# An HGRN recurrence with capacity-limited experts behind it: gathers, scatters, zero blocks and copied blocks in another order

## The chip, the core and the metric

The kernel runs on one core of one Trainium2 chip. The metric is the time of one execution on the device in microseconds, the median of several runs; lower is better. TensorE (PE) multiplies matrices, VectorE (DVE), ScalarE (ACT) and GpSimd (POOL) work elementwise, and SyncE (SP) issues most of the transfers. Each engine takes its own instructions in the order of the program and waits at semaphores for the others. Sixteen DMA engines carry every transfer between HBM (DRAM) and SBUF; PSUM is where TensorE writes.

## What is computed

The reference, cut to what matters. B, S, D = 4, 5056, 256, so N = 20224 tokens; E = 8 experts, F = 1024, capacity 80.

```python
sig = 1 / (1 + exp(-f_logit))
f = lower_bound + (1 - lower_bound) * sig
h = 0
for t in range(S):                     # per batch row and channel
    h = f[:, t] * h + (1 - f[:, t]) * x[:, t]
    y[:, t] = h
x = y.reshape(B * S, D)
logits = x @ w_gate
expert_idx = argmax(logits, axis=1)
gate_w = softmax(logits)[expert_idx]   # of each token, its own expert's
out = zeros((N, D))
for e in range(E):
    tok_idx = where(expert_idx == e)
    if len(tok_idx) > capacity:
        tok_idx = the capacity tokens with the largest gate_w
    out[tok_idx] = gate_w[tok_idx] * (relu(x[tok_idx] @ w1[e]) @ w2[e])
```

So at most 640 of the 20224 rows of the output are not zero; the other rows must be written as zeros.

## The kernel before

The first stage goes over 40 units of tokens (10 groups of 512 in each of the 4 batch rows). A unit loads 512 KB of `f_logit` and 512 KB of `x` into two of the eight ring slots (`ring`, 128x1024 f32 each), ScalarE takes the sigmoid, GpSimd multiplies it with `x` (`enter`), TensorE turns both, VectorE scans along time into `h_all`, which stays in SBUF whole, and TensorE makes the logits. In between, `copied` and `clear` write zeros to the output: `clear(source)` sends a tile of zeros from SBUF to the next 512 KB of `out`, `copied()` copies the first 512 KB of `out`, already zero, to the next 512 KB of `out`. One `clear(early)` and eleven `copied()` belong to this stage.

The second stage selects: VectorE and ScalarE rank candidates of each expert, TensorE counts and places them, and `trow` holds the token numbers of 8 x 80 slots. While it runs, SP brings the first seven halves of weights and writes more zeros. A half is 512 KB, half of `w1[e]` or of `w2[e]`, and takes slots 1 to 7 of the ring in turn (`half`); the order of the halves is `halves_of`. A half can be loaded once the half that lies seven before it in the order has been used up by TensorE.

The third stage, `experts`, is an order written out by hand; no planner moves anything. In it:

- `gather(e)` copies the 80 columns of `h_all` of expert e into `X[e]`, 24 on VectorE, 32 on ScalarE, 24 on GpSimd, each after loading the token numbers into the engine's registers; the tile pool `xp` has three buffers. `scaled(e)` multiplies `X[e]` on GpSimd.
- `hidden(e)` is 64 products with the two halves of `w1[e]` into two PSUM tiles; `relu(e, ps)` brings one to SBUF on ScalarE and one on VectorE; `result(e)` is 64 products with the two halves of `w2[e]`, and VectorE copies the result into `turned_y`, a band of 384 columns.
- `more(1)` issues two halves, and before `again` a `copied()` behind each half while blocks are left.
- `read_slots` loads slot numbers and gate values from DRAM, `rows_of` is a chain of 14 small VectorE instructions that makes from them the output rows (`goal`) and the factors (`gates`).
- `finish(t)` turns 128 columns of `turned_y` back (TensorE) and multiplies them by `gates` (VectorE) into `rows[0]`, which lies in ring slot 0; `scatter(t)` is an indirect DMA from GpSimd that writes these 128 rows to `out`. There are five (NT = 5).

The loop in short, with `finish` and `scatter` as soon as their rows are there but not ahead of e = 3 and e = 5:

```python
for e in range(E):
    if e and e + 2 < E: gather(e + 2)
    if e + 1 < E: ps = hidden(e + 1); relu(e + 1, ps); more(1)
    result(e); more(1)
    if e and e + 2 < E: scaled(e + 2)
    # e == 1: read_slots   e == 3: rows_of   then finish(..), scatter(..)
```

The branch `tc.If(unsure > 0)` at the end does the selection again in full and is not entered with these inputs.

Of the kernel before, what the change touches and what calls it, by code (L numbers as in the profile page):

```python
# [26 lines left out]
def kernel(  # L27
# [59 lines left out]
    def slot(i, name):  # L87
        return ring[i].tile([P, R * D], F32, name=name, tag="buf")
# [77 lines left out]
    with tc.tile_pool(name="gsm", bufs=1) as gsm:  # L166
# [228 lines left out]
        with tc.tile_pool(name="plg", bufs=1, space=PSUM) as plg, \  # L395
             tc.tile_pool(name="plt", bufs=1, space=PSUM) as plt:
            with tc.tile_pool(name="pss", bufs=2, space=PSUM) as pss, \
                 tc.tile_pool(name="psu", bufs=3, space=PSUM) as psu:
                for n in range(-AHEAD, n_unit):
                    unit(load, n + AHEAD)  # L400
                    m = n + AHEAD
                    if m == 1:
                        small_loads()
                    if m == 3:
                        clear(early)
                    elif 3 < m < TURN and m % 4 == 3:
                        copied()
                    elif m == n_unit - 1:
                        for _ in range(3):
                            copied()  # L410
                    unit(gate, n + 2)
                    if n == 0:
                        scaled_gate()
                    unit(enter, n + 2)
                    unit(turn_s, n + 1)
                    unit(turn_u, n + 1)
                    if n == n_unit - 2:
                        exponentials(0, LAST - 1)
                    unit(decay, n + 1)
                    unit(scan, n)  # L420
                    if n > 1 and n % B == 1:
                        aside(n // B - 1)
                    if n == n_unit - 3:
                        assert len(jobs) == 4
                    some_of(1 if n < TURN or n >= n_unit - 3 else 2 if n < n_unit - 1 else 0)
                    if n == n_unit - 2:
                        exponentials(LAST - 1, LAST)
                        summed(0, 4)
                        valued(0, 4, nc.gpsimd)
                    unit(logits, n - 1)  # L430
                    if n > 0 and n % B == 0:
                        g = n // B - 1
                        jobs.append(lambda g=g: by_token(g))
                        if g % 2 or g >= LAST - 1:
                            g0 = g - 1 if g < LAST - 1 else g
                            jobs += [lambda g0=g0, g=g: shifted(g0, g + 1),
                                     lambda g0=g0, g=g: equals(g0, g + 1),
                                     lambda g0=g0, g=g: choice(
                                         g0, g + 1, nc.gpsimd if g < LAST - 1 else nc.vector)]
# [48 lines left out]
                nc.vector.match_replace(out=src, in_to_replace=top, in_values=src,  # L488
                                        imm_value=NONE)

    order = [(1, 0), (2, 0), (1, 1)]
    for e in range(1, E):
        order += ([(1, e + 1)] if e + 1 < E else []) + [(2, e)]
    halves_of = [(which, e, i) for which, e in order for i in range(2)]
    used = [0]
# [19 lines left out]
        return t  # L515

    w_sb = {}
    SELECTING = 14
    for k, key in enumerate(halves_of[:NSLOT - 1]):
        if k % 2:  # L520
            copied()
        w_sb[key] = half(*key)
    for _ in range(SELECTING):
        copied()

    def columns_of(pool, at):
        ids = pool.tile([P, at.shape[1]], F32, name="ids")
# [175 lines left out]
    def experts(again):  # L703
        with tc.tile_pool(name="xp", bufs=3) as xp, \
# [7 lines left out]
            late = list(halves_of if again else halves_of[NSLOT - 1:])  # L712
            X, HID = {}, {}
            turned_y = yp.tile([P, DC, YR], F32, name="turned_y")
            rows = []

            def gather(e):
                X[e] = xp.tile([P, DC, K], F32, name="xe", tag="xe")
# [74 lines left out]
                nc.vector.tensor_scalar_mul(rows[0][:, t % R], t_ps, gates[:, ds(t, 1)])  # L793

            def scatter(t):
                nc.gpsimd.indirect_dma_start(  # L796
                    out=out, out_offset=bass.IndirectOffsetOnAxis(ap=goal[:, ds(t, 1)], axis=0),
                    in_=rows[0][:, t % R], in_offset=None, bounds_check=N - 1, oob_is_err=False)

            def more(m):  # L800
                for _ in range(2 * m):
# [13 lines left out]
                busy(psm, 5, "total")  # L815
            gather(1)
            scaled(1)
            ps = hidden(0)
            relu(0, ps)
            more(1)  # L820
            gather(2)
            scaled(2)
            if not again:
                total = psm.tile([1, 4], F32, name="total", tag="total")
                nc.tensor.matmul(total, ones, doubts[:, :4], start=True, stop=True)
            done = put_out = 0
            for e in range(E):
                if e and e + 2 < E:
                    gather(e + 2)
                if e + 1 < E:  # L830
                    ps = hidden(e + 1)
                    relu(e + 1, ps)
                    more(1)
                result(e)
                more(1)
                if e and e + 2 < E:
                    scaled(e + 2)
                if e == 1 and not again:
                    read_slots()
                    found = consts.tile([1, 1], F32, name="found")  # L840
                    nc.vector.tensor_reduce(found, total, AX.X, ALU.add)
                    nc.vector.tensor_copy(doubt, found)
                if e == 3 and not again:
                    rows_of(consts)
                while e >= 3 and (done + 1) * P <= (e + 1) * K:
                    finish(done)
                    done += 1
                while e + 3 >= E and put_out < done:
                    scatter(put_out)
                    put_out += 1  # L850
            assert put_out == NT
# [93 lines left out]
```

## Time and profile before

| what | value |
|---|---|
| median of 3 runs | 230.9 us (229.79 to 231.42) |
| the profiled execution | 230.06 us |
| its span, first to last instruction | 228.3 us |
| granted TensorE clock, mean | 0.947 |
| busy in the span: PE, DVE, ACT, POOL | 179.4, 160.3, 133.5, 140.3 us |
| moved by DMA | 80.66 MB, mean 353 GB/s |

Times in the rows below are microseconds from the start of the span of that one execution. A name such as L747 is a line of the kernel. A busy time of an engine is the union of its instructions; a DMA share is the mean busy share of the 16 DMA engines.

### The profile page before, as it was taken

What the parts mean: (1) busy time and instruction counts of PE and PEld (TensorE: products, weight loads), DVE (VectorE), ACT (ScalarE), POOL (GpSimd) and SP (SyncE); (2) the same over time, 40 slices, a digit from 0 to 9 for tenths busy, and PEclk for the clock granted to TensorE, in tenths of its full rate; (3) what the DMA queues carried; (4) which work ended last, traced back from release to release, by engine and by line L of the source; (5) the groups of instructions that cost most, each with busy time, mean ns of one, the idle gap of its engine ahead of it and who ended that gap; (6) DMA issues with size and microseconds to landing.
All of it is one profiled execution on the core that took longest, in us unless ns stands there. A gap on an engine that the chain in (4) does not pass through costs nothing. (4 is left out here: it accounts for less than half of the span.)

```text
span 228.3 us, 7296 instructions
## 1 busy us (share of the span) xinstructions
PE 179.4 (79%) x2452; PEld 149.5 (66%) x2452; DVE 160.3 (70%) x404; ACT 133.5 (58%) x423; POOL 140.3 (61%) x283
## 2 busy tenths in 40 slices
PE   0699899989998999899989758888957554998500
PEld 0598687867877787678767524578947453987400
DVE  5289878999989998999899999555353414652200
ACT  4288878777977888879788433466653260240000
POOL 4868779788978896889786632566555160052311
PEclk9999999999999999999999988997999987799955
DMA  6999999999999999999999999998999999397110
GB/s 232 335 422 414 414 409 420 408 412 411 392 416 404 411 376 414 417 409 384 411 455 358 425 434 375 353 333 296 332 400 451 401 334 394 127 366 279 41 44 26
DMA packets 20727, 80.66 MB, mean 353 GB/s; under 512 B 4409, under 2 KB 4409, under 8 KB 20057
## 3 DMA queue, kind: packets, MB, share of 16 engines
q1 hardware_dynamic: 20440, 79.46, 89.5%
q0 software_dynamic: 240, 0.66, 0.8%
q8 instruction: 21, 0.34, 0.7%
q14 instruction: 26, 0.20, 0.3%
HBM read 78.92 MB, written 21.37 MB: 439 GB/s over the span
## 5 line engine op out<-in xcount | busy, mean ns | idle before, releaser
L239 POOL TENSOR_TENSOR x_t<-f_t,x_t 128x1024 f32<-128x1024 f32 x40 | 94.9, 2374 | 22.1 <-DMA x_t<-in_x_dram 11.8
L270 DVE TENSOR_TENSOR_SCAN h_all<-h_all,up 128x512 f32<-128x512 f32 (+1 forms) x80 | 96.0, 1244 | 8.8 <-PE up L253 4.2
L262 ACT ACTIVATE h_all<-sp,nomlb 128x512 f32<-128x512 f32 (+1 forms) x80 | 50.1, 677 | 14.8 <-PE sp L245 11.8
L245 PE MATMUL sp<-ident,f_t 128*128 128x128 f32 x320 | 46.0, 289 | 7.0 <-ACT f_t L235 5.6
L235 ACT ACTIVATE f_t<-f_t 128x1024 f32<-128x1024 f32 x40 | 42.4, 1059 | 12.4 <-DMA f_t<-in_f_logit_dram 9.5
L253 PE MATMUL up<-ident,x_t 128*128 128x128 f32 x320 | 45.1, 283 | 4.0 <-DVE h_all L270 2.9
L245 PEld LDWEIGHTS sp<-ident,f_t 128*128 128x128 f32 x320 | 36.4, 147 | 15.1 <-issue 12.7
L253 PEld LDWEIGHTS up<-ident,x_t 128*128 128x128 f32 x320 | 37.2, 145 | 6.9 <-DVE h_all L270 4.4
L725 ACT COPY xe<-h_all 128x2 f32 x256 | 25.4, 190 | 18.5 <-issue 11.5
L747 PE MATMUL h_ps<-xe,w_sb 128*64 128x80 f32 x512 | 28.1, 273 | 7.4 <-DMA w_sb<-in_moe_w_dram 5.4
L725 POOL COPY xe<-h_all 128x2 f32 x192 | 24.5, 189 | 15.1 <-PE kept L679 6.0
L747 PEld LDWEIGHTS h_ps<-xe,w_sb 128*64 128x64 f32 x512 | 26.6, 186 | 9.6 <-DMA w_sb<-in_moe_w_dram 4.3
L725 DVE COPY xe<-h_all 128x2 f32 x192 | 22.6, 173 | 12.9 <-issue 10.7
L283 PE MATMUL lg<-h_all,wg 128*32 128x128 f32 (+1 forms) x640 | 26.5, 282 | 0.6 <-ACT ls L292 0.6
L769 PE MATMUL y_ps<-hid,w_sb 128*64 128x80 f32 x480 | 21.5, 247 | 3.5 <-DMA w_sb<-in_moe_w_dram 3.5
L769 PEld LDWEIGHTS y_ps<-hid,w_sb 128*64 128x64 f32 x480 | 19.9, 149 | 4.2 <-DMA w_sb<-in_moe_w_dram 3.4
L283 PEld LDWEIGHTS lg<-h_all,wg 128*32 128x32 f32 x640 | 15.4, 108 | 7.0 <-issue 4.9
L729 POOL TENSOR_TENSOR xe<-xe,omlb 128x160 f32<-128x160 f32 x8 | 3.6, 454 | 23.6 <-DVE xe L725 17.2
L755 ACT ACTIVATE hid<-h_ps 128x320 f32<-128x320 f32 x8 | 3.5, 434 | 21.7 <-issue 16.5
L796 POOL DMA_INDIRECT out_dram<-y,goal x5 | 5.1, 1023 | 12.7 <-DMA out_dram<-y,goal 11.9
L782 DVE COPY turned_y<-y_ps 128x160 f32<-128x160 f32 (+1 forms) x7 | 2.2, 318 | 14.5 <-PE y_ps L769 14.5
L307 PE MATMUL lt<-ident,ls 128*128 128x128 f32 (+1 forms) x40 | 7.5, 310 | 4.3 <-ACT ls L292 4.3
(132 smaller groups left out, 113.9 us busy)
## 6 DMA issues: line engine op xcount, KB each, us to landing
f_t<-in_f_logit_dram SPq DMA_DIRECT2D x40, 512.0 KB, 6.9
x_t<-in_x_dram SPq DMA_DIRECT2D x40, 512.0 KB, 7.1
out_dram<-out_dram SPq DMA_DIRECT2D x38, 512.0 KB, 10.2
w_sb<-in_moe_w_dram SPq DMA_DIRECT2D x31, 512.0 KB, 7.4
out_dram<-h_all SPq DMA_DIRECT2D x1, 512.0 KB, 8.9
w_sb<-in_moe_w_dram SPq DMA_DIRECT2D x2, 256.0 KB, 5.2
out_dram<-out_dram SPq DMA_DIRECT2D x1, 256.0 KB
out_dram<-y,goal POOLq DMA_INDIRECT x5, 3.5
```

What stands on the lines that cost most here:

```text
L235: nc.scalar.activation(s_t, s_t, ACT.Sigmoid, scale=-1.0)
L239: nc.gpsimd.tensor_tensor(u_t, sts[n], u_t, ALU.mult)
L245: nc.tensor.transpose(ps[:, ds(r * P, P)], sts[n][:, r, ds(o * P, P)], ident)
L253: nc.tensor.transpose(ps[:, r::R], uts[n][:, r, ds(o * P, P)], ident)
L262: nc.scalar.activation(columns(n, o).rearrange("p (k r) -> p k r", r=R), sps.pop((n, o)).rearrange("p (r k) -> p k r", r=R)[:, P - run(n / ...
L270: nc.vector.tensor_tensor_scan(h, h, ups.pop((n, o)), h_all[:, o, ds(spot(n - B) + G - 1, 1)] if n >= B else 0.0, ALU.mult, ALU.add)
L283: nc.tensor.matmul(lgs[g][ds(q * LC, LC), b, :k].rearrange("p (m i) -> p m i", i=2), wg[:, o], pairs[:, :, q], start=o == 0, stop=o == DC ...
L307: nc.tensor.transpose(lts[g0][:k, g - g0, j], ls[:, j::R], ident)
L725: copy(X[e][:, :, ds(k + j, 1)], h_all[:, :, ds(v, 1)])
L747: nc.tensor.matmul(h_ps[ds(s * H, H), c], wo[o][:, at:at + J * (H - 1) + 1:J], xt[:, o], start=o == 0, stop=o == DC - 1, skip_group_check= ...
L769: nc.tensor.matmul(ys[o][ds(s * H, H)], halves[c // CH][:, c % CH, ds(o * P + s * H, H)], hid[:, c], start=c == 0, stop=c == FC - 1, skip_ ...
L796: nc.gpsimd.indirect_dma_start(out=out, out_offset=bass.IndirectOffsetOnAxis(ap=goal[:, ds(t, 1)], axis=0), in_=rows[0][:, t % R], in_offs ...
```

## The change

- `gather` runs one expert further ahead: `gather(2)` and `scaled(2)` stand before `hidden(0)`, and in the loop `gather(e + 3)`, `scaled(e + 3)` stand between `hidden(e + 1)` and `result(e)`. `relu(e)` opens the turn of the loop in place of following `hidden(e)` at once.
- `scatter`: the scatters are told not to depend on each other; the last one depends on all others.
- `read_slots` and the flag for the branch move from e = 1 to e = 0, `rows_of` and the first `finish` from e = 3 to e = 2, the first scatters from e = 5 to e = 4.
- Zeros: GpSimd fills `zbuf` (ring slot 0) with zeros at the end of the first stage. The seven first halves are followed by one `copied()` each, and behind the second of them twelve `clear(zbuf)` are put in. Before, three `copied()` stood between the halves and fourteen behind them.
- The order of the halves: `w1[1]` ahead of `w2[0]`; the rest is as before.

```diff
--- before.py
+++ after.py
@@ -415,6 +415,8 @@
                     unit(turn_s, n + 1)
                     unit(turn_u, n + 1)
                     if n == n_unit - 2:
+                        zbuf = slot(0, "zbuf")
+                        nc.gpsimd.memset(zbuf, 0.0)
                         exponentials(0, LAST - 1)
                     unit(decay, n + 1)
                     unit(scan, n)
@@ -488,8 +490,8 @@
                 nc.vector.match_replace(out=src, in_to_replace=top, in_values=src,
                                         imm_value=NONE)
 
-    order = [(1, 0), (2, 0), (1, 1)]
-    for e in range(1, E):
+    order = [(1, 0)]
+    for e in range(E):
         order += ([(1, e + 1)] if e + 1 < E else []) + [(2, e)]
     halves_of = [(which, e, i) for which, e in order for i in range(2)]
     used = [0]
@@ -515,13 +517,13 @@
         return t
 
     w_sb = {}
-    SELECTING = 14
+    RANKING = 12
     for k, key in enumerate(halves_of[:NSLOT - 1]):
-        if k % 2:
-            copied()
         w_sb[key] = half(*key)
-    for _ in range(SELECTING):
         copied()
+        if k == 1:
+            for _ in range(RANKING):
+                clear(zbuf)
 
     def columns_of(pool, at):
         ids = pool.tile([P, at.shape[1]], F32, name="ids")
@@ -712,7 +714,7 @@
             late = list(halves_of if again else halves_of[NSLOT - 1:])
             X, HID = {}, {}
             turned_y = yp.tile([P, DC, YR], F32, name="turned_y")
-            rows = []
+            rows, sent = [], []
 
             def gather(e):
                 X[e] = xp.tile([P, DC, K], F32, name="xe", tag="xe")
@@ -793,9 +795,17 @@
                 nc.vector.tensor_scalar_mul(rows[0][:, t % R], t_ps, gates[:, ds(t, 1)])
 
             def scatter(t):
-                nc.gpsimd.indirect_dma_start(
+
+                sent.append(nc.gpsimd.indirect_dma_start(
                     out=out, out_offset=bass.IndirectOffsetOnAxis(ap=goal[:, ds(t, 1)], axis=0),
-                    in_=rows[0][:, t % R], in_offset=None, bounds_check=N - 1, oob_is_err=False)
+                    in_=rows[0][:, t % R], in_offset=None, bounds_check=N - 1, oob_is_err=False))
+                for other in sent[:-1]:
+                    if t < NT - 1:
+                        tc.declare_no_dep(sent[-1].ins, other.ins, reason="other rows")
+                    else:
+                        tc.add_manual_dep(sent[-1].ins, other.ins.name, mybir.DependencyInfo(
+                            mybir.DependencyClass.Sync, mybir.DependencyReason.DATA),
+                            reason="all rows")
 
             def more(m):
                 for _ in range(2 * m):
@@ -815,37 +825,36 @@
                 busy(psm, 5, "total")
             gather(1)
             scaled(1)
-            ps = hidden(0)
-            relu(0, ps)
-            more(1)
             gather(2)
             scaled(2)
+            ps = hidden(0)
+            more(1)
             if not again:
                 total = psm.tile([1, 4], F32, name="total", tag="total")
                 nc.tensor.matmul(total, ones, doubts[:, :4], start=True, stop=True)
             done = put_out = 0
             for e in range(E):
-                if e and e + 2 < E:
-                    gather(e + 2)
+                relu(e, ps)
                 if e + 1 < E:
                     ps = hidden(e + 1)
-                    relu(e + 1, ps)
                     more(1)
+                if e + 3 < E:
+                    gather(e + 3)
+                    scaled(e + 3)
                 result(e)
                 more(1)
-                if e and e + 2 < E:
-                    scaled(e + 2)
-                if e == 1 and not again:
+                if e == 0 and not again:
                     read_slots()
                     found = consts.tile([1, 1], F32, name="found")
                     nc.vector.tensor_reduce(found, total, AX.X, ALU.add)
                     nc.vector.tensor_copy(doubt, found)
-                if e == 3 and not again:
-                    rows_of(consts)
-                while e >= 3 and (done + 1) * P <= (e + 1) * K:
+                if e == 2:
+                    if not again:
+                        rows_of(consts)
+                while e >= 2 and (done + 1) * P <= (e + 1) * K:
                     finish(done)
                     done += 1
-                while e + 3 >= E and put_out < done:
+                while e + 4 >= E and put_out < done:
                     scatter(put_out)
                     put_out += 1
             assert put_out == NT
```

## Rows read from the trace of the kernel before

**Rows 1.** Stretches: busy us (count) of PE, PEld, DVE, ACT, POOL; clock, DMA share, GB/s.
```profile
100.00:116.00 16.00, 15.48 (x196) 13.19 (x196) 14.84 (x15) 12.94 (x19) 12.51 (x7) 1.00 1.02 402
138.00:154.00 16.00, 13.99 (x144) 9.32 (x142) 10.76 (x76) 7.69 (x72) 7.96 (x54) 0.96 1.01 346
154.00:168.00 14.00, 13.09 (x256) 12.86 (x256) 7.23 (x53) 9.11 (x86) 7.49 (x51) 0.88 0.91 331
175.00:182.00 7.00, 3.16 (x78) 2.70 (x76) 2.51 (x18) 3.22 (x32) 2.77 (x23) 1.00 1.04 428
195.00:200.00 5.00, 5.00 (x119) 5.00 (x116) 3.23 (x25) 1.65 (x14) 0.45 (x1) 0.78 0.28 95
```

**Rows 2.** Waits of SP's queue: who waited for whom, us, times, longest.
```profile
SPq L513 <- PE h_ps L747: 10.0, 2, 7.2
```

**Rows 3.** Timeline of SP's issues: start, us, engine, line, operation, names, count.
```profile
114.22 1.78 SPq L141 DMA_DIRECT2D out_dram<-out_dram  x3
...
190.36 7.94 SPq L513 DMA_DIRECT2D w_sb<-in_moe_w_dram  x2
...
200.28 5.67 SPq L513 DMA_DIRECT2D w_sb<-in_moe_w_dram  x5
```

**Rows 4.** Timeline of TensorE and ScalarE around expert 5; idle before in brackets.
```profile
186.87 3.46 PE L769 MATMUL y_ps<-hid,w_sb 128*64 128x80 f32 x48 [1.96 <-DMA w_sb<-in_moe_w_dram]
...
193.62 0.62 PE L791 MATMUL t_ps<-ident,turned_y 128*128 128x128 f32 x2 [2.91 <-DVE y L793]
...
194.17 3.85 PE L747 MATMUL h_ps<-xe,w_sb 128*64 128x80 f32 x64
...
198.79 3.36 ACT L725 COPY xe<-h_all 128x2 f32 x32 [1.69 <-issue]
...
201.00 2.44 PE L747 MATMUL h_ps<-xe,w_sb 128*64 128x80 f32 x64
```

**Rows 5.** Timeline of the last experts and the scatters.
```profile
208.64 2.38 PE L769 MATMUL y_ps<-hid,w_sb 128*64 128x80 f32 x64
...
211.92 0.48 DVE L793 TENSOR_SCALAR y<-t_ps,gates 128x256 f32<-128x256 f32 x1 [0.53 <-PE t_ps L791]
...
213.94 0.31 PE L769 MATMUL h_ps<-hid,w_sb 128*64 128x80 f32 x4
...
214.94 0.48 DVE L793 TENSOR_SCALAR y<-t_ps,gates 128x256 f32<-128x256 f32 x1 [0.54 <-PE t_ps L791]
...
219.59 0.97 POOL L796 DMA_INDIRECT out_dram<-y,goal  x1 [3.42 <-DMA out_dram<-y,goal]
223.17 0.97 POOL L796 DMA_INDIRECT out_dram<-y,goal  x1 [2.60 <-DMA out_dram<-y,goal]
```

**Rows 6.** The chain that ended last: start, us, what.
```profile
215.20 3.62 DMA out_dram<-y,goal
```

**Rows 7.** The page's DMA issues: engine, operation, count, KB each, median us to landing.
```profile
out_dram<-out_dram SPq DMA_DIRECT2D x38, 512.0 KB, 10.2
...
w_sb<-in_moe_w_dram SPq DMA_DIRECT2D x2, 256.0 KB, 5.2
...
out_dram<-y,goal POOLq DMA_INDIRECT x5, 3.5
```

**Rows 8.** Timeline of GpSimd: a memset at the start, and the end of stage one.
```profile
1.65 1.02 POOL L203 MEMSET h_all<- 128x1024 f32 x1
...
125.21 1.21 POOL L355 TENSOR_TENSOR cand<-cand 128x256 f32<-128x256 f32 x2 [1.63 <-ACT cand L343]
```

**Rows 9.** Timeline of the first experts.
```profile
154.71 4.38 PE L747 MATMUL h_ps<-xe,w_sb 128*64 128x80 f32 x64 [1.02 <-POOL xe L729]
...
155.99 3.13 ACT L725 COPY xe<-h_all 128x2 f32 x32 [1.59 <-issue]
...
158.88 2.74 PE L769 MATMUL y_ps<-hid,w_sb 128*64 128x80 f32 x64
```

**Rows 10.** The tile of the weights: landings of its loads.
```profile
DMA to landing us min/median/max: 4.5/7.1/10.7
```

## The prediction

> **What bounds the kernel now.** I read the table by stretches first. In 100 to 116, as in 138 to 154 and 175 to 182, the sixteen DMA engines are the limit, with a busy share of 1.0; behind 138 no compute engine but TensorE comes near it [rows 1]. Three things there matter. Where only copies of `out` into `out` run (138 to 154) the queue is as busy but moves 346 GB/s, against 402 for loads and 428 for weights and copies mixed. From 154 to 168 the share falls to 0.91. From 195 to 200 it is 0.28. The waits of SP's queue say why the last happens: a half of `w2` waited 7.2 us for `hidden` to give its ring slot back [rows 2]; it stands in the timeline as the pair of issues that took from 190.36 to 198.30 [rows 3]. The engines' timeline shows what held that `hidden`: TensorE stands in order, `result(3)` ended at 190.33, the transposes of `finish(1)` came at 193.62 after a wait of 2.91 for VectorE's first product, which in the code stands behind the chain of `rows_of`, and `hidden(5)` came at 194.17 [rows 4]. Last, the end: the last product of the experts ends at 214.25, and the five scatters go one after the other to 224.14 [rows 5]; a step of the chain of waits is the landing of the one before, 215.20 to 218.82 [rows 6]. So there are three limits in order of time: DMA bandwidth, then the ring of slots with the order on TensorE, then a serial chain of scatters up to 228.3.
>
> **The change part by part.** *The scatters.* Before, each waits for the landing of the one ahead, 3.58 to 4.39 us from start to start [rows 5, 6]. After, t = 0 to 3 wait for no scatter, t = 0 to 2 are issued an expert earlier, and the last waits for all. Held against the old times of the products: the rows of t = 3 are multiplied by 212.40, so with 0.2 us allowed for the hand-over its scatter starts at 212.6; 3.5 us to landing [rows 7] make 216.1; 0.77 from a landing to the next start (218.82 to 219.59) and the last starts at 216.9 in place of 223.17. Its own rows are there at 215.42, so the added wait costs some 1.3 us beside a scatter without one; nothing is queued behind it on GpSimd but the end. Gain 6.3; 5.8 with a landing as long as 4.1 us, 7.5 if the wait cost nothing. What follows the start of the last scatter, 223.17 to 228.3, stays. Were the scatters still serial, the earlier place alone would let three of them end before t = 3 is due, so this term stands on two legs.
>
> *The zeros.* In both kernels 39.5 blocks of 524,288 B are written, 12 of them ahead of the first weights. The other 27.5 are 3 + 14 + 10.5 copies before; after, 7 copies (one behind each of the first seven halves), 12 clears from `zbuf` and 8.5 copies. A block costs 524,288 B over the rate [rows 1]: 1.52 us for copies alone, 1.30 for loads, 1.22 mixed. No row shows clears in a row. Lower bound 1.22, since nothing went through the queue faster over a stretch; upper bound 1.52, a copy, which writes the same bytes and reads them too. I take 1.30, as a clear crosses between SBUF and HBM once, as a load does; the ends move the sum by -1.0 and +2.6. What 138 to 154 moved, 16 x 346 = 5.5 MB, would take 13.8 us at 402: gain 2.2. And as two more blocks go out before the experts start, two copies fewer stand between their weights.
>
> The Trainium skill ("DMA: Bandwidth & Descriptors", Where 436 GB/s comes from) speaks against this gain: it says that between HBM and SBUF a core's share of the HBM, some 358 GB/s, binds. By that a clear would cost 1.46 us (an estimate from the page) and the sum would come out 1.9 us later. The trace does not agree for loads, at 402 GB/s on this one core [rows 1].
>
> *The fill of `zbuf`.* One memset of 128x1024 on GpSimd, behind the last product into `x_t`. The same shape took 1.02 us, and GpSimd stands idle for 1.63 us just there, until ScalarE's exponentials let it go on at 125.21 [rows 8]: nothing on the path; without that cover, 1.0 us on the selection. SP waits for it with the clears and the next five halves behind: it would reach the first clear at about 120 and stands until some 124.6. A copy takes 10.2 us from issue to landing [rows 7], so what was issued by 119 keeps the DMA engines busy to about 129, and they do not run dry. Of those halves the first wanted are `w1[1]`: 129, 12 clears (15.6) and three blocks (3.9) make 148.5, six ahead of `hidden(1)` at 154.71 [rows 9]. So the swap of `w2[0]` and `w1[1]` costs nothing.
>
> *Gathers one expert ahead.* `gather(e+3)` waits for the buffer of `X[e]`, free once `hidden(e)` ends. An expert costs ScalarE 1.69 for registers, 3.36 for 32 columns [rows 4] and one `relu` of under half a microsecond: 5.5 us, eight times from about 146, so to 190, and `hidden(7)` is not wanted before some 196. Behind each gather stand `relu(e+1)` on ScalarE and VectorE, and on VectorE the copy of `y`, for which TensorE's next `result` waits. `relu(0)` moves behind `gather(2)`, which ended at 159.12; without a `relu` ahead it ends some 0.4 sooner, so `relu(0)` is done at 159.2, where `result(0)` started at 158.88 [rows 9]: +0.3, in a stretch where DMA has slack. If cover is gone, the price is one gather, 5.5.
>
> *The order of the rest.* `read_slots` moves from e = 1 to e = 0, `rows_of` and `finish(0)` from e = 3 to e = 2. VectorE's chain then runs behind `result(2)`, where TensorE waits for weights anyway, and one set of transposes, not two, stands ahead of a `hidden`, so none waits for VectorE's product. Of the 3.84 us between `result(3)` and `hidden(5)` [rows 4] that removes some 2.8. It is not added by itself: it shows as the queue's idle time at 195.
>
> *The queue's sum.* The idle time of 154 to 168 is 0.09 x 14 = 1.3 us, that of 195 to 200 is 0.72 x 5 = 3.6 [rows 1]. With the 2.2 above, 7.1. A count from the other side: the last three copies of the first stage were issued by 116.0 [rows 3], the middle one at about 115.4 landing (10.2) at 125.6; behind it come 32 halves and 27.5 blocks, at 1.30 together 77.4 us, so the last weights land at 203.0 in place of some 210.8 (issued near 205.6 [rows 3], 5.2 to landing [rows 7]): 7.8. I take 8, near the count, since the table's stretches leave out 182 to 195. TensorE stood 3.4 us behind the last landing, because `result(6)` ended only at 211.02 [rows 5]; with products in time it should stand a `result` behind, 2.4: 1 more. Together 9.
> What is late next: `hidden(e)` frees a slot, and a half needs at least 4.5 us from issue to landing [rows 10], with three halves (3.9 us) queued meanwhile. So a gap of some 0.6 us in a round, and one fall of the clock: +1.
>
> *Sum.* -6.3 - 9 + 1 = -14.3 on the profiled execution's own 230.06 (its span is 228.3, 1.8 lie around it), so 215.8. The median of the runs is 0.8 above that execution: I say 216.5, with a span of about 214.
>
> **The rivals.** *Only the tail is won.* The queue's gain is lost: clears cost what copies cost, and the ring, not bandwidth, paces the experts, TensorE freeing slots too late as at 195. For it: seven slots hold less than two experts, and SP waited for `h_ps` while DMA stood idle [rows 1, 2]. Against: that wait has a cause which the change takes out. It gives 230.06 - 6.3 + 0.8 = 224.6.
>
> *The clock stays down (the slower case).* The granted clock was 0.88 in 154 to 168 and 0.78 in 195 to 200 [rows 1], a mean of full clock and of its lower level, behind waits of TensorE. Were experts 4 to 7 to run wholly at 1.2 GHz, each `hidden` (2.44 [rows 4]) and `result` (2.38 [rows 5]) would take twice as long: 9.6 us a round in place of the 5.2 that four halves take on the queue, so 4.4 x 4 = 17.6 more, and the time 234. It decides once a round outlasts the queue by 3.6. Against: `hidden(6)`, just behind a wait, took 2.44, and the waits left in a round are some 0.5 us, with one of 3 ahead of `hidden(4)`.
> The Trainium skill ("TensorE: Matmul & The Clock Gate", HAM oscillation) describes just this, a wait for DMA in each tile that puts the clock down every time. The trace agrees in part: the clock fell twice among the experts, but never stayed down for a whole one.
>
> *It does nothing.* The scatters are held by the zeros and not by each other, and as many bytes go through the queue: 231. Against: the start at 219.59 follows the landing of the one ahead, at 218.82, and no zeros are under way by then [rows 5, 6].
>
> **How the numbers follow.** The forecast, 212 to 220: 0.68 (the bounds of a clear, of a landing and of the hidden gathers). Only the tail, 220 to 227: 0.22. Clock down, over 232: 0.05. Nothing: 0.05. To leave out no more than 2 in 10 the range goes on to 225. The three runs lie 0.7% apart, so under 1% cannot be told from no change. Faster 0.90, same 0.05, slower 0.05.
>
> **What will show it.** Right: three scatters started by about 195, the last some 2 to 3 us behind the last product; in 138 to 154 over 390 GB/s; no stretch of share 0.28; the last weights landed by 204. Wrong: under 370 GB/s while clears run, SP waiting over 3 us for `h_ps`, a granted clock under 0.8 through the last four experts, or the copy of `y` late behind VectorE's last gather.

## The result and the profile after

The changed kernel takes 219.05 us (median of four runs, 217.37 to 220.39) against 231.16 for the kernel before beside it (229.79 to 231.42): a ratio of 0.9484, interval 0.9396 to 0.9572. Forecast were 216.5 and a range of 212 to 225. Some executions of one and the same kernel take a few per cent longer than its others; medians and ratios here are of the others. The profiled execution took 217.37, with a span of 215.6; against the 230.06 and 228.3 of before that is 12.7 less, where the sum said 14.3.

First the table by stretches of the changed kernel, with the columns of [rows 1]:

```profile
116.00:138.00 22.00, 17.01 (x173) 11.73 (x170) 20.97 (x47) 13.88 (x32) 14.06 (x23) 0.93 1.01 412
138.00:154.00 16.00, 13.33 (x149) 9.26 (x148) 9.79 (x72) 6.83 (x67) 7.61 (x52) 0.99 1.04 426
154.00:168.00 14.00, 13.07 (x260) 12.57 (x256) 10.12 (x77) 9.73 (x95) 9.87 (x73) 0.88 0.98 389
175.00:182.00 7.00, 3.95 (x94) 3.49 (x95) 3.68 (x21) 3.22 (x33) 3.23 (x24) 1.00 0.99 390
195.00:200.00 5.00, 4.03 (x87) 3.51 (x88) 0.46 (x2) 0.44 (x1) 1.44 (x2) 1.00 0.89 318
200.00:206.00 6.00, 4.66 (x116) 4.21 (x112) 0.59 (x2) 0.44 (x1) 0.00 (x0) 1.00 0.57 198
```

In 138 to 154 the queue moves 426 GB/s in place of 346, and the stretch of share 0.28 is gone: 0.89. What is new is the 0.57 behind 200, and that TensorE, at full clock, is busy for only 4.0 of the 5 us of 195 to 200, where before it had no idle time. The timeline of TensorE there (start, us, what ran, idle before in brackets):

```profile
186.48 0.44 PE L793 MATMUL t_ps<-ident,turned_y 128*128 128x128 f32 x2 [0.42 <-DVE turned_y L784]
186.85 2.44 PE L749 MATMUL h_ps<-xe,w_sb 128*64 128x80 f32 x64
...
192.27 2.46 PE L749 MATMUL h_ps<-xe,w_sb 128*64 128x80 f32 x61
195.02 0.37 PE L749 MATMUL h_ps<-xe,w_sb 128*64 128x80 f32 x3 [0.30 <-issue]
195.23 0.32 PE L771 MATMUL y_ps<-hid,w_sb 128*64 128x80 f32 x2
195.81 0.38 PE L771 MATMUL y_ps<-hid,w_sb 128*64 128x80 f32 x4 [0.25 <-issue]
196.55 0.41 PE L771 MATMUL y_ps<-hid,w_sb 128*64 128x80 f32 x5 [0.37 <-issue]
197.29 2.21 PE L771 MATMUL y_ps<-hid,w_sb 128*64 128x80 f32 x53 [0.34 <-issue]
199.33 2.39 PE L749 MATMUL h_ps<-xe,w_sb 128*64 128x80 f32 x64
...
204.46 0.91 PE L771 MATMUL y_ps<-hid,w_sb 128*64 128x80 f32 x18 [0.92 <-issue]
...
208.27 0.31 PE L771 MATMUL h_ps<-hid,w_sb 128*64 128x80 f32 x4
```

The stall of 2.91 ahead of the transposes [rows 4] is gone: they start at 186.48 and `hidden(5)` at 186.85, 7.3 us earlier. But `hidden(6)` and `result(5)` took 7.0 us, 192.27 to 199.3, where two such groups need 4.8 [rows 4, 5]: behind 61 products TensorE gets them by twos to fives, one batch in some 0.73 us, and the word in the brackets is "issue", a wait for nothing that the profile names. A second stall, 0.92, stands in `result(6)`. I had forecast neither.

The timeline of GpSimd's scatters:

```profile
192.96 1.22 POOL L799 DMA_INDIRECT out_dram<-y,goal  x1 [0.77 <-DMA w_sb<-in_moe_w_dram]
194.48 0.98 POOL L799 DMA_INDIRECT out_dram<-y,goal  x1 [0.30 <-issue]
195.76 0.98 POOL L799 DMA_INDIRECT out_dram<-y,goal  x1 [0.30 <-issue]
207.01 0.97 POOL L799 DMA_INDIRECT out_dram<-y,goal  x1 [10.28 <-DVE y L795]
210.22 0.97 POOL L799 DMA_INDIRECT out_dram<-y,goal  x1 [2.24 <-DVE y L795]
```

Three are issued in a row by 196, and the last starts 1.6 us behind the last product (208.58); before it was 8.9 behind (214.25 to 223.17) [rows 5]. So the 12.7 us are 5.7 by which the products end earlier and 7.3 by which the last scatter stands nearer behind them, less 0.3 behind it (5.4 to the end of the span, before 5.1).

### The profile page after: what moved, and what is told of

It reads as the page before. It is cut to its first block, busy times and chain, and to the rows that moved or that the text cites. A ratio compares the mean times of both kernels' runs of the same rounds, so it can differ in the third digit from the quotient of the medians.

```text
span 215.6 us, 7313 instructions
## 1 busy us (share of the span) xinstructions
PE 177.4 (82%) x2452; PEld 146.8 (68%) x2452; DVE 158.4 (73%) x404; ACT 132.6 (62%) x423; POOL 141.5 (66%) x284
## 4 chain that ended last, share of the span: by engine, by line
PE 35%; DMA 22%; ACT 14%; issue 12%; DVE 10%; SPq 2%; POOL 1%; ACTq 1%; POOLq 0%; DVEq 0%
PE sp L245 12%; DMA w_sb<-in_moe_w_dram 11%; PE up L253 9%; PE lg L283 7%; DMA f_t<-in_f_logit_dram 6%; ACT h_all L262 6%; ACT xe L727 4%; DMA lb<-in_lower_bound_dram 3%; DVE h_all L270 3%; PE lt L307 3%; ACT ls L292 2%; PE y_ps L771 2%; PE h_ps L749 2%; POOL out_dram L799 1%; DVE at L632 1%
## 5 line engine op out<-in xcount | busy, mean ns | idle before, releaser
L245 PE MATMUL sp<-ident,f_t 128*128 128x128 f32 x320 | 45.5, 287 | 7.0 <-ACT f_t L235 5.6
L245 PEld LDWEIGHTS sp<-ident,f_t 128*128 128x128 f32 x320 | 36.0, 145 | 15.1 <-issue 12.7
L727 ACT COPY xe<-h_all 128x2 f32 x256 | 25.4, 191 | 18.8 <-issue 10.3
L749 PE MATMUL h_ps<-xe,w_sb 128*64 128x80 f32 x512 | 27.1, 264 | 6.5 <-DMA w_sb<-in_moe_w_dram 5.0
L749 PEld LDWEIGHTS h_ps<-xe,w_sb 128*64 128x64 f32 x512 | 25.5, 178 | 8.5 <-DMA w_sb<-in_moe_w_dram 4.2
L771 PEld LDWEIGHTS y_ps<-hid,w_sb 128*64 128x64 f32 x480 | 18.7, 138 | 5.5 <-issue 4.6
```

The lines of the kernel that those rows point to most:

```text
L245: nc.tensor.transpose(ps[:, ds(r * P, P)], sts[n][:, r, ds(o * P, P)], ident)
L727: copy(X[e][:, :, ds(k + j, 1)], h_all[:, :, ds(v, 1)])
L749: nc.tensor.matmul(h_ps[ds(s * H, H), c], wo[o][:, at:at + J * (H - 1) + 1:J], xt[:, o], start=o == 0, stop=o == DC - 1, skip_group_check= ...
L771: nc.tensor.matmul(ys[o][ds(s * H, H)], halves[c // CH][:, c % CH, ds(o * P + s * H, H)], hid[:, c], start=c == 0, stop=c == FC - 1, skip_ ...
```

## The experiments

Two questions: what is each part worth, and where does TensorE's shortage of instructions come from? For the second there were two theories. **L** (loads): TensorE's instructions are themselves fetched through the DMA engines, and a fetch queued behind weights comes late. **S** (scatters): the scatters issued in a row take something from TensorE. Each ratio is to the kernel before on the same chip; the first four runs shared a chip, as did the four f and the three g.

**The parts one at a time.** The scatters alone:

```diff
-                nc.gpsimd.indirect_dma_start(
+                sent.append(nc.gpsimd.indirect_dma_start(
...
+                for other in sent[:-1]:
+                    if t < NT - 1:
+                        tc.declare_no_dep(sent[-1].ins, other.ins, reason="other rows")
+                    else:
+                        tc.add_manual_dep(...)
```

> The kernel before with only the scatters freed of each other (the last still waits for all), in their old places. Theory 1, the chain of scatters held the end by itself: last scatter starts near 216.9 in place of 223.2, the time falls by 6.3, ratio 0.973. Rival, the scatters are held by the products or by something else on GpSimd: under 2 us, ratio over 0.99.

Measured: 0.9835 (0.9774 to 0.9895), 225.45 against 228.84; expected was 0.973. In its trace the last scatter starts at 216.60, 6.6 earlier than in the trace of before, as the term said. But here the three scatters in a row (205.67, 207.19, 208.47) fall into `hidden(7)` and `result(6)`, and TensorE's timeline shows the same small batches:

```profile
207.22 0.37 PE L769 MATMUL y_ps<-hid,w_sb 128*64 128x80 f32 x5
207.75 0.41 PE L769 MATMUL y_ps<-hid,w_sb 128*64 128x80 f32 x5 [0.16 <-issue]
```

`result(6)` took 4.5 us in place of 2.38 [rows 5]. These 2 us are lost already within the 6.6. The medians differ by 3.4 only; the profiled execution, 223.82, is the fastest of the four, and the rest of the gap stays unexplained.

The zeros alone (the fill of `zbuf`, the 12 clears and the fewer copies):

```diff
+                        zbuf = slot(0, "zbuf")
+                        nc.gpsimd.memset(zbuf, 0.0)
...
-    SELECTING = 14
+    RANKING = 12
...
-        if k % 2:
-            copied()
...
-    for _ in range(SELECTING):
...
+        if k == 1:
+            for _ in range(RANKING):
+                clear(zbuf)
```

> The kernel before with only the zeros changed: zbuf filled, twelve clears, a copy behind each of the first seven halves. Theory 1, clears cost 1.25 us in place of 1.5 and two copies fewer stand among the weights, but TensorE still stalls ahead of hidden(5) and the scatters still go one by one: 2 to 4 us less, ratio 0.983 to 0.991. Rival, the experts are paced by ring slots and TensorE: no change, ratio 0.997 to 1.003, with more idle DMA.

Measured: 0.9927 (0.9887 to 0.9968), a gain of 1.6 us, under the 2 to 4 of theory 1; 138 to 154 moves 419 GB/s. The faster queue is there, but with the old order of the experts not all of it reaches the end: the transposes ahead of `hidden(5)` still wait 3.03 us for VectorE, at 191.04.

The order alone (gathers one expert ahead, order of halves, `read_slots`, `rows_of` and `finish` an expert earlier; scatters issued earlier but still one after the other, zeros as before):

```diff
-                if e and e + 2 < E:
-                    gather(e + 2)
...
+                if e + 3 < E:
+                    gather(e + 3)
+                    scaled(e + 3)
...
-                while e + 3 >= E and put_out < done:
+                while e + 4 >= E and put_out < done:
```

> The kernel before with only the order of the experts changed (gathers one ahead, relu, rows_of, finish and the place of the scatters, order of the halves); old zeros, scatters still one after the other. Theory 1: the stall ahead of hidden(5) goes (3 to 5 us) and three scatters are over before the last two are due, so most of the tail is won too: 8 to 11 less, ratio 0.952 to 0.965. Rival, the serial chain keeps the end: 3 to 5 less, ratio 0.978 to 0.987.

Measured: 0.9735 (0.9675 to 0.9796), 222.99; between the two expectations. The three gains, 3.4, 1.6 and 5.9, add up to 10.9; the whole change gained 12.1 and, run again below, 10.3. Within the spread of the runs the parts add, and the interval of each lies below 1.

**The changed kernel with the scatters serial again.**

```diff
-                for other in sent[:-1]:
-                    if t < NT - 1:
-                        tc.declare_no_dep(sent[-1].ins, other.ins, reason="other rows")
-                    else:
-                        tc.add_manual_dep(...)
```

> The changed kernel with its scatters waiting for each other as before. Theory 1, the earlier place alone wins the tail, since three scatters of about 4 us each from 193 on are over by 205, before the fourth is due at 207: within 1 us of the changed kernel, ratio to the kernel before 0.945 to 0.955. Rival, freeing them is what counts: 4 us or more slower than the changed kernel, ratio 0.965 or more. If the stall of TensorE near 195 comes from three scatters at once, this run is up to 3 us faster than the changed kernel.

Measured: 0.9611 (0.9561 to 0.9661), 220.86; again between. The timeline of its scatters says why:

```profile
194.13 1.21 POOL L798 DMA_INDIRECT out_dram<-y,goal  x1 [0.77 <-DMA w_sb<-in_moe_w_dram]
200.66 0.97 POOL L798 DMA_INDIRECT out_dram<-y,goal  x1 [5.32 <-DMA out_dram<-y,goal]
206.91 0.97 POOL L798 DMA_INDIRECT out_dram<-y,goal  x1 [5.28 <-DVE turned_y L784]
```

From start to start they stand over 6 us apart, not the 3.6 to 4.4 of before [rows 5, 6]: a scatter issued while weights are queued lets the next one start late. So t = 0 to 2 do not end before t = 3 is due, and the last starts at 214.46, 5.2 behind the last transposes (209.24), where the changed kernel, run again, has 1.4 (208.60 to 209.97).

**The changed kernel again, and with the old zeros.** The second turns the zeros back:

```diff
-                        zbuf = slot(0, "zbuf")
-                        nc.gpsimd.memset(zbuf, 0.0)
...
-    RANKING = 12
+    SELECTING = 14
...
+        if k % 2:
+            copied()
...
+    for _ in range(SELECTING):
...
-        if k == 1:
-            for _ in range(RANKING):
-                clear(zbuf)
```

> The changed kernel once more, beside the runs of this group. Both theories: ratio to the kernel before 0.940 to 0.957, with TensorE short of instructions for about 3 us in expert 5 (products in small batches, idle time put down to issue).

> The changed kernel with the zeros as before: three copies between the first seven halves, fourteen behind them, no zbuf. Theory 1, copies alone take 1.5 us and clears 1.25, and two more blocks stand among the weights: 2 to 4 us slower than the changed kernel. Rival, the zeros are hidden by the selection and by the ring of slots: within 1 us of the changed kernel.

Measured: 0.9536 (0.9468 to 0.9604), 218.35, with the small batches again (195.30 to 197.50), and 0.9603 (0.9511 to 0.9694), 220.55. In this company the zeros are worth 2.2 us by the medians; the intervals overlap, so this alone does not show it. Old zeros give 357 GB/s in 138 to 154 again.

**Scatters spaced out** to one behind each `finish`, so that no three stand in a row:

```diff
-                while e + 4 >= E and put_out < done:
+                while e >= 2 and put_out < done:
```

> The changed kernel with each scatter issued right behind its finish: t = 0 at e = 2, t = 1 at e = 3, t = 2 at e = 4, in place of all three at e = 4. Theory S, three scatters issued one behind the other on GpSimd starve TensorE of instructions: the small batches vanish, the end comes 2 to 3 us sooner than in the changed kernel, ratio near 0.937. Theory L, TensorE's instructions come by a 16 KB load that stands behind the queued weights, whatever the scatters do: the stall of 2 to 3 us stays in expert 5, ratio within 0.5% of the changed kernel.

Measured: 0.9492 (0.9385 to 0.9599), 217.07. `hidden(6)` (194.56, 2.46) and `result(5)` (196.83, 2.41) ran without a gap. From the start of `hidden(5)` to the end of the last product it took 18.7 us, in place of 21.7 (21.2 in the changed kernel run again). Its fetch of instructions, told below, came in time. But `hidden(5)` started at 189.09, two later than in the changed kernel run again, with a granted clock of 0.64 in 181 to 189 (there 0.85), and the last scatter at 209.43 against 209.97. The stall went, as S expected and L did not; the time stayed within 0.5%, as L expected and S did not. Not shown to be faster.

**Only two scatters**, t = 0 to 2 left out:

```diff
-                    scatter(put_out)
+                    if again or put_out >= 3:
+                        scatter(put_out)
```

> The changed kernel without the scatters of t = 0 to 2: 384 of the 640 rows are not written to the output (left at zero), the last two scatters stay. Theory S: no stall in expert 5, last product 3 us sooner than in the changed kernel, time about 3 us less. Theory L: the 16 KB load for expert 6 still starts some 3 us behind its place and the stall stays, time within 1 us.

Measured: 0.948 (0.9386 to 0.9574), 217.88, within half a us of the run with all five. TensorE's timeline:

```profile
196.16 1.82 PE L771 MATMUL y_ps<-hid,w_sb 128*64 128x80 f32 x47
199.90 0.78 PE L771 MATMUL y_ps<-hid,w_sb 128*64 128x80 f32 x17 [1.92 <-issue]
```

With no scatter near, TensorE still stands for 1.92 us in the midst of `result(5)`: as one gap, not in batches. So a shortage needs no scatter. The same gap, at the same place behind 47 products, is in three runs whose scatters are not in a row: 1.81 in e4 (at 199.38), 2.75 in e3 and 1.90 in g3 (told below):

```profile
202.45 1.36 PE L769 MATMUL y_ps<-hid,w_sb 128*64 128x80 f32 x17 [2.75 <-issue]
```

```profile
199.20 0.78 PE L771 MATMUL y_ps<-hid,w_sb 128*64 128x80 f32 x17 [1.90 <-issue]
```

The table of the DMA queues shows what this gap waits for. One queue, q8, carries packets of 16 KB marked as instructions; between those at 102.20, 112.04 and 123.82 of the kernel before TensorE ran some 240 to 260 products and weight loads each time, so I take it for TensorE's. Its rows are there only for a stretch in which a fetch starts (queue, kind: packets, MB, share of 16 engines). The first is 193.9 to 197.4 of f4, the second 197.4 to 198.4; `hidden(6)` started at 193.89.

```profile
q1 hardware_dynamic: 423, 1.30, 101.3%
...
q1 hardware_dynamic: 194, 0.38, 98.8%
q8 instruction: 1, 0.02, 5.8%
```

One fetch of 16 KB starts at 197.63 and ends at 198.55 (the times of its packet in the trace); TensorE goes on at 199.90. The profile page of the changed kernel counts 21 such fetches (0.34 MB). How far a fetch lies behind its `hidden` differs. In the four runs with the gap it starts 3.5 to 4.4 us behind (f4 as told, g3 193.21 and 196.67, e4 193.44 and 197.10, e3 195.61 and 199.99), and TensorE resumes 1.3 to 1.5 us behind its end. In the kernel before it starts 1.1 and 1.3 behind (`hidden(6)` 201.00 and 202.07, `hidden(7)` 206.37 and 207.62) and in f3 1.3 (194.56 and 195.84), and no gap follows. Weights were queued there too (share 1.02 in 201.0 to 206.4 before), so a busy queue alone does not make a fetch late; how much must be queued, and for how long, no run separates.

The small batches are not such a late fetch. In f2 the fetch lay at 199.10 to 199.98 and in e1 at 205.01 to 205.94, in time, and the batches came all the same. In f2:

```profile
200.65 0.36 PE L769 MATMUL y_ps<-hid,w_sb 128*64 128x80 f32 x3 [0.16 <-issue]
201.37 0.37 PE L769 MATMUL y_ps<-hid,w_sb 128*64 128x80 f32 x5 [0.37 <-issue]
```

In all four runs that have them (e1, f1, f2 and the changed kernel) the stalls that part them begin and end with the scatters: TensorE resumes for the first time 0.5 to 0.6 us behind the start of the second of three in a row, for the last time some 0.5 behind the end of the third. There TensorE's semaphore signals come late as well: that of the last product of `hidden(6)` in the changed kernel 2.1 us behind the product's end (195.39 and 197.49, the time of the update in the trace), in f4 within 0.03. So f4 speaks against S for the gap, but not for the batches.

**Fewer instructions.** If L holds, a product with half as many instructions should need fewer fetches:

```diff
-                    for s in range(2):
-                        nc.tensor.matmul(
-                            ys[o][ds(s * H, H)], halves[c // CH][:, c % CH, ds(o * P + s * H, H)],
-                            hid[:, c], ...)
+                    nc.tensor.matmul(ys[o], halves[c // CH][:, c % CH, ds(o * P, P)],
+                                     hid[:, c], ...)
```

> The changed kernel with the second product of an expert made of 32 products with 128 columns of weights in place of 64 with 64: the same sums, 64 instructions fewer on TensorE in an expert of some 256. Theory L, TensorE runs short because its 16 KB load comes late behind queued weights: with a quarter fewer instructions the gaps put down to issue in experts 5 and 6 shrink to under 1 us, and the time falls by 1 to 2 us, ratio near 0.945, unless the wide products are slower. Theory S, the scatters starve TensorE: small batches and gaps of 2 to 3 us stay, time as in the changed kernel.

and the same for `hidden` too:

```diff
-                            for s in range(2):
-                                at = i * FH + a * J * P + j + J * s * H
...
+                            at = i * FH + a * J * P + j
+                            nc.tensor.matmul(
+                                h_ps[:, c], wo[o][:, at:at + J * (P - 1) + 1:J], xt[:, o], ...)
```

> As the run with wide second products, and the first products of an expert wide as well: half the instructions on TensorE. Theory L: no gap put down to issue in experts 5 to 7, 1 to 3 us less than the changed kernel. Theory S: gaps stay. If wide products take over 76 ns from one to the next (twice the 37 of narrow ones), TensorE gets slower by that and the queue waits for slots.

Measured: 0.9657 (0.9601 to 0.9712), 222.31, and 1.1944 (1.1889 to 1.1998), 273.63. g1 has no gap for instructions and no batch, though its three scatters stand in a row (196.08 to 199.86), but it does not answer the question, since a wide product costs more than two narrow ones: 32 in 3.80 us against 64 in 2.38. g2 is told at the end.

**Spaced scatters, the last one free too.** Beside the edit of the spaced ones:

```diff
-                    if t < NT - 1:
+                    if True:
```

> The changed kernel with each scatter right behind its finish and the last not waiting for the others. Theory 1: the last scatter starts when its rows are there, some 0.5 us sooner, and the small batches are gone: 0.5 to 2 us less than the changed kernel, ratio 0.940 to 0.950. Rival, a landing is as long as the wait it replaces, two scatters at once land later: no difference.

Measured: 0.9516 (0.947 to 0.9561), 218.24. The last scatter starts 1.2 behind the last transposes (207.84 to 209.09), where with the wait it was 1.4: its wait for the others costs next to nothing. And though its scatters are spaced as in f3, g3 has the gap of 1.90 shown above: spacing takes the batches away, not the late fetch.

**No weights queued.** The loads of the weights of experts 6 and 7 are left out and those of expert 5 used again, so that the queue is empty from some 194.6 on, with the three scatters still in a row:

```diff
+            late = [key for key in (halves_of if again else halves_of[NSLOT - 1:])
+                    if again or key[1] < 6]
...
-                wo = [w.pop((1, e, o)) for o in range(DC)]
+                wo = [w[1, e if again else min(e, 5), o] for o in range(DC)]
...
-                halves = [w.pop((2, e, i)) for i in range(2)]
+                halves = [w[2, e if again else min(e, 5), i] for i in range(2)]
```

> The changed kernel without the loads of the weights of experts 6 and 7, which are computed with expert 5's halves instead (their 160 rows are wrong); gathers, products and scatters stay. Theory L: the DMA queue is empty from about 192, so the 16 KB loads of TensorE's instructions start within some 1.5 us of each hidden and no stall is left behind them; the last product comes 4 to 6 us sooner than in the changed kernel (no weights to wait for), time 212 to 214. Theory S: three scatters in a row still break TensorE's products of expert 5 into small batches for 2 to 3 us, whatever the queue holds; time 214 to 216.

Measured: 0.9424 (0.9366 to 0.9482), 216.24. TensorE's timeline, and two of its scatters:

```profile
195.06 2.44 PE L750 MATMUL h_ps<-xe,w_sb 128*64 128x80 f32 x64
197.32 2.38 PE L772 MATMUL y_ps<-hid,w_sb 128*64 128x80 f32 x64
199.54 2.38 PE L750 MATMUL h_ps<-xe,w_sb 128*64 128x80 f32 x64
201.75 2.38 PE L772 MATMUL y_ps<-hid,w_sb 128*64 128x80 f32 x64
```

```profile
197.28 0.97 POOL L800 DMA_INDIRECT out_dram<-y,goal  x1 [0.30 <-issue]
198.56 0.97 POOL L800 DMA_INDIRECT out_dram<-y,goal  x1 [0.30 <-issue]
```

No gap and no batch, though the scatters start in the midst of the products. The fetches start ahead of their `hidden`: 194.66 and 199.38, for 195.06 and 199.54. From `hidden(5)` to the last product it takes 17.7 us. Together with f4 this settles the gap: it needs queued weights and no scatter. The batches need scatters in a row (e3, e4, f3, f4 and g3 have none) and did not come with the queue empty. That it is the fetch in particular which the gap waits for is read from the traces' packets, not tried by itself; what holds TensorE in the batches is open. The time itself, 216.24, lies above what either theory expected. The lag was there before anything that the edit touches: `hidden(0)` started at 151.52 in place of 148.49, behind a stretch at the lower clock (0.50 in 141 to 147; TensorE had idled 2.65 and 2.08 us ahead of it), and the second part of `hidden(4)` at 182.97 in place of 180.62.

## Why the prediction was right, and where a term was off

**The scatters: right in size, one of its two legs false.** Forecast 6.3 less; the last scatter stands 7.3 nearer behind the last product. But I said that the earlier place alone would do it. By e4 it doesn't: a serial scatter among queued weights takes over 6 us from start to start. The landing of 3.5 from [rows 7] is a median of scatters most of which had the queue to themselves. Freeing them counts by the traces, the last scatter being 5.2 and 1.4 behind the last transposes; by the ratios it is 0.9611 (e4) and 0.9536 (f1), whose intervals overlap. And the 1.3 that I put on the last one's wait for the others is hardly there (1.2 without it in g3, 1.4 with it).

**The zeros: right.** I took 1.30 us for a clear between 1.22 and 1.52; in the changed kernel they land 1.20 to 1.32 apart, and 116 to 138 moves 412 GB/s, 1.27 a block. The 358 GB/s of the Trainium skill ("DMA: Bandwidth & Descriptors", Where 436 GB/s comes from), by which a clear would cost 1.46 (an estimate from the page), did not bind on this one core. The fill of `zbuf` took 0.96 at 122.50, and GpSimd was then still idle for 0.75 until the exponentials released it at 124.21, so the cover held. SP waited 4.4 us for it, where the forecast was 4.6 (120 to 124.6), and the share of the DMA engines stayed at 1.01:

```profile
SPq L155 <- POOL zbuf L419: 4.4, 1, 4.4
```

**The gathers: hidden, as costed.** `result(0)` starts at 158.42; before 158.88 [rows 9], with `hidden(0)` 1.0 earlier than before: 0.5 later, where I said 0.3. No `hidden` waited for a gather from expert 2 on.

**The clock: the rival did not come.** The granted clock was 1.00 in every stretch from 168 to 206, so the fall for which I had put some 1 us did not come there either. I had read two falls among the experts of the kernel before; there were three (0.50 in 156.2 to 159.6, 187.0 to 190.3 and 193.8 to 197.1). A slow product is not always the clock: at 1.00 `hidden(0)` took 4.07 us (148.49), `hidden(2)` 4.00 (160.80) and `hidden(3)` 3.83 for 60 products (169.38), where `hidden(5)` took 2.44. In `hidden` the weights of experts 0 to 3 are read with a column step of 4, those of 4 to 7 with 2 (`rows_of_w2`); that this is the reason no run tries.

**"Only the tail"** would have been 224.6 and did not come either.

**The queue: right in mechanism, too large in size.** This is the term that was off. The products end 5.7 earlier, where my terms for the queue and what is late next made 8. The count of blocks put the last weights at 203.0; they landed at 205.16. And I let TensorE stand 2.4 behind them; it stands 3.4, as before. Both misses have the size of the shortage: 7.0 - 4.8 = 2.2 us in `hidden(6)` and `result(5)`, and 0.92 in `result(6)`, which stands behind a fetch of 202.03 to 202.99. For the first the trace shows the way to the weights. SP's queue had two halves to load into the slots of `w1[6]`, and waited from 191.99 to 197.49 for TensorE's signal, 2.1 behind the last product of `hidden(6)`:

```profile
191.55 8.25 SPq L515 DMA_DIRECT2D w_sb<-in_moe_w_dram  x5
```

```profile
SPq L515 <- PE h_ps L749: 8.7, 3, 3.5
...
SPq L515 <- remote: 5.5, 1, 5.5
```

It is the wait of 5.5; the view calls its releaser "remote", as no product ends close ahead of it. My sign for "wrong", a wait of over 3 us for `h_ps`, came too, but elsewhere: the 3.5 ended at 182.95, behind `hidden(4)`, which itself had waited 1.98 for weights, and is half of the 7.2 of before [rows 2].

The 2.2 and 0.92 outdo the 2.3 by some 0.8, and against them stands 1.0 that was there already when `hidden(0)` started (148.49, before 149.50), which the change does not explain. So what came late next was not the ring by itself, as I wrote, but TensorE's instructions and signals: my term of +1 for it should have been some 3. Before, the queue had stood at a share of 0.28 in 195 to 200, and the next fetch was only 1.1 late; that a fuller queue makes it later fits this, but no run turns that alone.

That the sum missed the profiled execution by 1.6 only is in part luck: the queue fell 2.3 short, the scatters gave 1.0 more than their term, and the 1.0 at `hidden(0)` helped.

**Open.** What holds TensorE in the small batches: they came with three scatters in a row and weights queued at their start (e1, f1, f2 and the changed kernel), and not with an empty queue (h1). But g1 had both and no batch, and in e1 they went on while the queue ran out (share 0.36 in 207.6 to 210.0). No version is shown to beat the changed kernel. From `hidden(5)` to the last product it took 21.7 and 21.2 us, f4 with the gap 20.3, f3 with neither gap nor batches 18.7; in f3 the lower clock around expert 4 took part of this back.

## What to carry to other kernels

Price a transfer by rows with the same company on the queue: a scatter that lands in 3.5 us at the quiet end held up the next one for over 6 among loads, so serial chains of small transfers get dearer, not cheaper, when moved to a busier place. When a DMA queue is filled to the brim, count the program itself as one of its customers: a long unrolled run of products needs fetches of instructions, and here they started up to 4.4 us behind their group among queued loads. A gap put down to "issue" in the midst of a group is the sign to look for them, and for indirect scatters issued beside it.

## What the runs showed of the hardware that was not expected

**A fetch of instructions can wait behind data**: told above, 0.2 to 0.4 us ahead of its `hidden` with an empty queue (h1), 3.5 to 4.4 behind it in the four runs with a gap, and up to 2.75 us of TensorE's time (e3).

**Scatters in a row can hold TensorE**: told above, products in batches of two to six, one in some 0.73 us, and signals up to 2.7 us behind the products' ends (e1: 207.44 and 210.07, f1: 194.93 and 197.60). Beside a single scatter they were 0.7 to 0.8 late (e4: 194.77 and 195.47, f3: 195.89 and 196.72), and in h1, with no weights queued, within 0.03.

**A busy TensorE at the lower clock.** g2, with both products wide, ran from 151 us to the end at half clock. Ahead of that it had not idled for more than 0.7 us at a time since 139, and in 151 to 180 it was busy for 29.00 of 29 us. Its table by stretches, columns of [rows 1]:

```profile
180.00:220.00 40.00, 39.58 (x184) 39.37 (x183) 13.53 (x94) 9.65 (x88) 8.99 (x66) 0.50 0.52 187
220.00:262.00 42.00, 41.20 (x193) 40.77 (x193) 3.20 (x9) 0.87 (x2) 4.27 (x5) 0.50 0.30 100
```

and one of its products:

```profile
206.74 7.03 PE L769 MATMUL y_ps<-hid,w_sb 128*128 128x80 f32 x32
```

TensorE was busy for 39.58 of 40 and 41.20 of 42 us, and the granted clock stayed at 0.50, 1.2 GHz. A product over 128 columns takes 7.03 / 32 = 0.22 us there; in g1, 3.80 / 32 = 0.12, which is three times the 2.38 / 64 = 0.037 of a narrow one, for twice the columns. What put the clock down in g2 and not in g1 was not tried.
